# Two feed-forward layers on one Trainium2 core: sums taken off GpSimd, and the last two pairs of units multiplied with eight products

## The chip, the cores and the metric

The kernel runs on one core of one Trainium2 chip. The metric is the device time of one execution in microseconds (us). Before the change, three runs took 548.48, 549.16 and 550.05 us; the median is 549.16 us. A measurement of this kernel tells a change from no change at about 0.3%, 1.6 us.

The engines are named as the profile names them: PE is TensorE's matmul and PEld its weight load, DVE is VectorE, ACT is ScalarE, POOL is GpSimd, SP is SyncE, which issues the plain DMAs. The DMAs that add to their destination are issued by POOL.

## The reference

What is computed is causal attention over 2 x 12 heads of 448 positions and 64 channels, then two feed-forward layers over the 896 tokens (d_model 768, d_ff 2048). The weights arrive as 8-byte floats.

```python
x = attention(q, k, v)                      # causal, softmax, (896, 768)
h = x @ moe_w_in;  x = (h * cos(h)) @ moe_w_out
h = x @ moe2_w_in
g = where(h >= 1, h, where(h <= -1, 0, (h + 1) ** 2 / 4))
out = g @ moe2_w_out
```

## The kernel before, in words

**Order of work.** Attention follows a hand-written list of steps (STEPS). Then come four feed-forward stages: stage 1, `stage_in_plain` (x @ moe_w_in, plain products); stage 2, `stage_out(0)` (first moe_w_out); stage 3, `stage_in_split` (moe2_w_in); stage 4, `stage_out(1)` (second moe_w_out, whose results are the output, stored transposed). The class `Steps` records every operation of these stages with its engine, an assumed cost and the buffers that it reads and writes; `Plan.run` searches 300 rounds for an order and then emits the instructions of all engines in that order. Each engine and each queue runs its own instructions strictly in the emitted order. TensorE's order is the one in which the products are recorded.

**Products.** Every f32 operand is split into a high part in fp32r (ACT, `cast`, line 709 or, negated, 711) and a low rest (DVE, `rest`, line 718 or, negated, 720); one product is three matmuls per 128 rows: high-high, high-low, low-high. Stages 2 to 4 use a scheme with seven block products in place of eight, for which sums of blocks of the weights and of the activations are formed first. Stages 2 and 4 have 28 products of 18 matmuls each (7 products, `p`, times 4 slices, `j`), line 1013. Stage 3 walks over eight pairs of units g = 0..7 (128 columns of d_ff each); a pair has seven products of 9 matmuls, line 1275. Stages 2, 3 and 4 have 504 matmuls each, all of 128x128 by 448 columns.

**Weights.** A unit or a row block of 768 KB is loaded by SP into a raw buffer (line 333 or 807). ACT turns the top 16 bits of every weight into fp16 (`decode_top`, line 347); DVE joins them with the next bits to an f32 word (`decode_bits`, line 357), for units in place, in every second word of the raw buffer (`middle`). Half of each decoded row block is then negated on POOL (`minus`, line 821).

**Sums.** Those on POOL use `combine` (line 703): in stage 3 four sums S1 to S4 of 128x384 per pair (`sums` in `group`); in stages 2 and 4 the activation sums T1 (stage 4 also T2 and T3) of 128x896 and the weight sums S1 of 128x768, one per slice; between stages 2 and 3 nine differences of 128x448 (`difference`: T1, T2, T3). T4 between the stages runs on DVE. The sums T2 to T4 and S2 to S4 that line 698 (`add_by_dma`) forms are DMAs that POOL issues and that add the source to the destination in SBUF.

**PSUM hand-overs.** Results are read out of PSUM by DVE (line 1050 in stages 2 and 4; line 703 with `g<-m,kept` in stage 3) or kept by ACT (lines 1039, 1287). A later product that accumulates in the same PSUM tile waits for such a read. The gate of stage 3 is two ACT operations (1305, 1308) and one on DVE (1311) for each 448 tokens.

**Buffers of stage 3.** Raw units turn over four slots (b3 to b6), so the load of pair g+2 waits for the last reader of pair g. The split weights of a pair lie in the slots w0 to w3, one of each.

```python
go((1, 0), (5, 0), (6, 0), (2, 0), (7, 0))              # pair 0: (product, pair)
early = [(3, g - 1), (6, g), (4, g - 1)]                # pairs 1 to 7
go((1, g), (2, g), *early, (5, g), (7, g))
```

## Time and profile before

| | |
|---|---|
| median of the runs | 549.16 us (548.48 to 550.05) |
| the profiled execution | 550.65 us, span of its instructions 548.9 us |
| PE, PEld busy | 517.1 us (94%), 445.4 us (81%) |
| DVE busy | 425.8 us (78%) |
| ACT busy | 350.8 us (64%) |
| POOL busy | 232.5 us (42%) |
| TensorE's granted clock, mean | 0.981 of 2.4 GHz |
| a 768 KB unit from issue to landing, median | 4.7 us |
| decode of a unit, mean | ACT 1.08 us, DVE 1.07 us |
| casts on ACT, mean | 0.89 us (128x768), 0.57 us (128x448), 0.54 us (128x384) |
| the chain that ended last | PE 66%, DVE 20%, issue 6%, ACT 5%, POOL 2% |

Busy shares are means over the span; matmuls are pipelined, so TensorE's pace is read from the starts of successive matmuls and not from its busy share. A timeline row merges neighbouring instructions of one kind; `[4.18 <-DVE c L1050]` says that the engine stood idle for 4.18 us before it and that the DVE instruction of line 1050 that writes `c` ended this. Instructions of ACT and DVE overlap by about 0.1 us at their ends, so a row's length is a little more than what it adds to the engine's time. In the view of busy times by stretch, (x86) counts instructions, PEclk is TensorE's granted clock as a share of 2.4 GHz.

### The profile page before, as it was taken

The numbers are of one execution on the slowest core, as the hardware profiler recorded it, in microseconds if no ns is written. First come the engines' busy times: TensorE is split into PE (matmuls) and PEld (weight loads), VectorE is DVE, ScalarE is ACT, GpSimd is POOL, SyncE is SP. The second block draws the span as 40 slices with busy tenths as digits, with TensorE's granted clock in tenths as the row PEclk, the third lists the DMA queues.
The fourth block names the chain that finished last, engine by engine and source line by source line (L and its number), as shares of the span: only waits on it lengthen the run. The fifth ranks groups of instructions, "written<-read, shape, count | busy, mean of one in ns | idle before, by whom it ended". The sixth has DMA issues, their size and how long they took to land.

```text
span 548.9 us, 7642 instructions
## 1 busy us (share of the span) xinstructions
PE 517.1 (94%) x2792; PEld 445.4 (81%) x2792; DVE 425.8 (78%) x518; ACT 350.8 (64%) x599; POOL 232.5 (42%) x238
## 2 busy tenths in 40 slices
PE   8999999999999999999988979999999978899997
PEld 4666779989898988989877968898888767799886
DVE  7879775776766465997699976879899899997652
ACT  5998975866765465545475558777877665644340
POOL 4856641121201017770167062546485867770000
PEclk9999999999999999999997989999999988899999
DMA  8753309799842565665330334333359464792111
GB/s 267 261 177 124 94 3 320 219 301 289 270 108 74 132 158 93 123 119 99 116 115 1 115 97 152 98 115 110 121 144 312 141 182 146 153 203 54 50 51 51
DMA packets 42405, 79.01 MB, mean 144 GB/s; under 512 B 2432, under 2 KB 31616, under 8 KB 42368
## 3 DMA queue, kind: packets, MB, share of 16 engines
q1 hardware_dynamic: 36464, 61.51, 33.8%
q0 software_dynamic: 5760, 16.78, 16.7%
q8 instruction: 22, 0.36, 0.3%
q10 hardware_dynamic: 144, 0.23, 0.1%
q14 instruction: 15, 0.12, 0.1%
HBM read 58.98 MB, written 2.75 MB: 112 GB/s over the span
## 4 chain that ended last, share of the span: by engine, by line
PE 66%; DVE 20%; issue 6%; ACT 5%; POOL 2%; DMA 1%; DVEq 0%; ACTq 0%
PE m L1013 25%; PE m L851 19%; PE m L1275 7%; PE o L544 4%; PE m L591 2%; PE sa L431 2%; POOL raw L703 2%; PE tx L518 2%; PE sb L431 1%; PE tz L518 1%; DVE raw L357 1%; PE tw L518 1%; DVE g1.3.1_3746 L1311 1%; DVE w1g L718 1%; ACT top L347 1%
## 5 line engine op out<-in xcount | busy, mean ns | idle before, releaser
L851 PE MATMUL m<-x,w 128*128 128x384 f32 (+2 forms) x516 | 105.3, 366 | 0.0
L851 PEld LDWEIGHTS m<-x,w 128*128 128x128 f32 x516 | 93.4, 188 | 11.6
L703 POOL TENSOR_TENSOR raw<-raw 128x384 f32<-128x384 f32 x24 | 40.0, 1668 | 49.4 <-DVE raw L357 31.7
L347 ACT CAST top<-raw 128x768 f16<-128x768 bf16 x32 | 34.6, 1082 | 10.2 <-DMA raw<-in_moe_w_in 8.3
L357 DVE SCALAR_TENSOR_TENSOR raw<-raw,top 128x768 uint32<-128x768 uint32 x32 | 34.1, 1065 | 8.7 <-ACT top L347 8.7
L1275 PE MATMUL m<-rx,w2g 128*128 128x448 f32 x144 | 32.6, 370 | 3.6 <-ACT kept L1287 1.3
L1275 PE MATMUL m<-rx,w0g 128*128 128x448 f32 x144 | 32.4, 378 | 3.3 <-DVE w0g L718 3.3
L1275 PE MATMUL m<-rx,w1g 128*128 128x448 f32 x144 | 32.0, 368 | 2.3 <-DVE g1.1.0_3225 L703 1.2
L1275 PEld LDWEIGHTS m<-rx,w2g 128*128 128x128 f32 x144 | 26.7, 189 | 8.1 <-ACT kept L1287 2.1
L1275 PEld LDWEIGHTS m<-rx,w0g 128*128 128x128 f32 x144 | 28.1, 196 | 5.9 <-DVE w0g L718 3.6
L1275 PEld LDWEIGHTS m<-rx,w1g 128*128 128x128 f32 x144 | 26.7, 188 | 5.9 <-issue 1.6
L703 POOL TENSOR_TENSOR c<-c,c 128x448 f32<-128x448 f32 x9 | 15.0, 1682 | 29.7 <-issue 25.2
L1050 DVE TENSOR_TENSOR c<-m,p 128x448 f32<-128x448 f32 x24 | 14.5, 617 | 15.7 <-PE m L1013 15.6
L498 POOL TENSOR_SCALAR p<-p,rb 128x256 f32<-128x256 f32 (+1 forms) x32 | 18.1, 577 | 19.8 <-DVE rb L484 14.8
L544 PE MATMUL o<-pT,v 128*64 128x448 f32 (+3 forms) x192 | 23.2, 385 | 0.9 <-ACT pT L535 0.9
L498 POOL TENSOR_SCALAR p<-p,ra 128x384 f32<-128x384 f32 (+1 forms) x48 | 22.1, 479 | 3.2 <-ACT p L476 1.2
L1287 ACT COPY kept<-m 128x448 f32<-128x448 f32 x24 | 12.6, 526 | 16.3 <-PE m L1275 14.3
L544 PEld LDWEIGHTS o<-pT,v 128*64 128x64 f32 x192 | 12.6, 136 | 12.0 <-issue 6.3
L709 ACT CAST rx<-c 128x448 fp32r<-128x448 f32 x20 | 10.8, 567 | 11.7 <-DVE c L1050 10.0
L718 DVE TENSOR_TENSOR w1g<-raw,w1g 128x768 fp32r<-128x768 f32 x8 | 13.6, 1704 | 3.5 <-ACT w1g L709 3.5
L476 ACT ACTIVATE p<-sb,nmb 128x256 f32<-128x256 f32 x24 | 11.2, 476 | 7.1 <-DVE nmb L457 4.1
L476 ACT ACTIVATE p<-sa,nma 128x384 f32<-128x384 f32 x24 | 13.8, 584 | 1.8 <-DVE nmd L455 1.1
(639 smaller groups left out, 1443.3 us busy)
## 6 DMA issues: line engine op xcount, KB each, us to landing
raw<-in_moe_w_in SPq DMA_DIRECT2D x32, 768.0 KB, 4.7
v<-in_v SPq DMA_DIRECT2D x12, 256.0 KB, 5.7
k<-in_k SPq DMA_DIRECT2D x12, 224.0 KB, 5.1
out<-c SPq DMA_DIRECT2D x12, 224.0 KB, 1.9
qr<-in_q SPq DMA_DIRECT2D x11, 224.0 KB, 5.2
...
```

Source lines behind the costliest of these rows:

```text
L347: nc.scalar.copy(out=top.bitcast(FP16).rearrange("p (m e) -> p m e", e=2)[:, :, 1], in_=raw.bitcast(BF16)[:, 4:].rearrange("p (m e) -> p m ...
L357: nc.vector.scalar_tensor_tensor(out=fl, in0=bits, scalar=13, in1=top, op0=ALU.logical_shift_right, op1=ALU.bitwise_or,)
L431: nc.tensor.matmul(s[:, j, o : o + w], self.q[rows(n, j), i * QB : w], self.k[rows(n, j), :w], start=(o == 0), stop=False,)
L476: nc.scalar.activation(out=o, in_=i, func=AF.Exp, bias=nm[:, m : m + 1], scale=1.0 if n else scale, accum_out=self.r[r][:, c : c + 1],)
L498: e.tensor_scalar(out=p, in0=p, scalar1=r[:, c : c + 1], scalar2=1.0, op0=ALU.mult, op1=ALU.mult)
L518: nc.tensor.transpose(o, i, ident)
L544: nc.tensor.matmul(self.o[heads(j), c * QB : S], self.v[:, j, c, :], self.pT[:, c, j, c * QB :], start=(c == 0), stop=(c == FULL),)
L703: make = lambda: e.tensor_tensor(out=to(), in0=a(), in1=b(), op=op)
L718: nc.vector.tensor_tensor(out=to(), in0=what(), in1=f32(hi()), op=ALU.subtract)
L851: nc.tensor.matmul(o, w[:, a, c * P : (c + 1) * P], x(t, c)[:, s], start=(c == first and n == 0), stop=(c == last and n == 2),)
L1013: nc.tensor.matmul(o, wt[:, a, i * MW + d * P : i * MW + (d + 1) * P], r[:, i], start=(p in (0, k, 2, 4) and j == 0 and i == 0 and n == 0) ...
L1275: nc.tensor.matmul(o, wt[:, l, block, c * P : (c + 1) * P], rt[:, s, x], start=(n in (1, 2, 5) and c == 0 and e == 0), stop=(c == ML - 1 a ...
```

## The change

1. No arithmetic on POOL in the feed-forward stages. T1, T2, T3 and S1 of stages 2 and 4 move to DVE. Of stage 3's four sums per pair two move to DVE (new S2, S3), and two become adding DMAs (S4, S1). The sums between stages 2 and 3 (T1 to T4) become one adding DMA each over 128x1344; for that `c21` and `c12` are stored negated, and the pieces made from them are split with a sign. `minus` goes: the top half of a row block is decoded by two ACT operations, the second with a factor of -1; the second unit of a pair is decoded negated.
2. Decoded words of units are packed into the first words of the raw buffer (`words`) and no longer lie in every second word; the two sums E0, E1 follow behind them.
3. The pairs 6 and 7 of stage 3 (`CLASSIC`) use eight products with R11, R12, R21, R22 and no sums (`plain_product`); three new pieces R12 and two new slots for them (e0, e1).
4. Products of pairs 1 to 5 come in a new order; a gate takes two blocks in one instruction where both are ready. Row blocks and sums of stage 4 get other slots; the buffer for the descriptors of POOL's DMAs shrinks to 4096 bytes.

```diff
+    def decode_top(top, raw, sign=1, half=None):
...
+        if sign > 0:
+            nc.scalar.copy(out=to, in_=what)
+        else:
+            nc.scalar.mul(out=to, in_=what, mul=-1.0)
...
-        plan.op(
-            f"{k}a{n}", "ACT", 1.08, lambda: decode_top(tops[1], tile_of(name)), [(name, 0)], [("top1", 0)],
-        )
+        for half, sign in enumerate((1, -1)):
+            plan.op(
+                f"{k}a{n}.{half}", "ACT", 0.66, lambda half=half, sign=sign: decode_top(tops[1], tile_of(name), sign, half),
+                [(name, 0)], [("top1", half)],
+            )
...
-        plan.op(f"{k}g{n}", "POOL", 0.75, minus, [(ws, (1, i))], [(ws, (1, i))])
...
         def g_combine(name, j, to, a, b, op):
             combine(
-                f"{k}{name}.{j}", "POOL", 2.3, lambda: g_part(k, j, to), lambda: g_part(k, j, a), lambda: g_part(k, j, b),
+                f"{k}{name}.{j}", "DVE", 1.1, lambda: g_part(k, j, to), lambda: g_part(k, j, a), lambda: g_part(k, j, b),
...
-                    f"{k}S1.{j}", "POOL", 2.0, lambda j=j: ws_part(k, j, 0), lambda j=j: ws_part(k, j, 0),
+                    f"{k}S1.{j}", "DVE", 0.96, lambda j=j: ws_part(k, j, 0), lambda j=j: ws_part(k, j, 0),
...
+    def sum_of(name, to, what):
+        add_by_dma(
+            f"1d{name}", lambda: tile_of(to), lambda: tile_of(what),
+            [(t, c) for t in (to, what) for c in range(ML)], [(to, c) for c in range(ML)],
+        )
...
-            for d in range(ML):
-                difference("T1", "c210", "c210", "c220", ALU.subtract, d)
+                piece("R12", d, "c210", -1)
+            sum_of("T1", "c210", "c220")
+            sum_of("T2", "c110", "c220")
...
-            for d in range(ML):
-                difference("T4", "c110", "c120", "c110", ALU.subtract, d, "DVE")
+            sum_of("T4", "c110", "c120")
...
         def sums():
-            for u in (u0, u1):
-                decode(u)
-            for name, to, x, y, op in (
-                ("S1", (a, "B0"), (b, "A1"), (b, "A0"), ALU.add), ("S3", (b, "B0"), (a, "A1"), (b, "A1"), ALU.subtract),
-                ("S2", (a, "B1"), (a, "B0"), (a, "A1"), ALU.subtract), ("S4", (b, "B1"), (a, "A0"), (a, "B1"), ALU.subtract),
-            ):
-                combine(f"1{name}g{g}", "POOL", 1.2, half(*to), half(*x), half(*y), op, [x, y], [to])
+            decode(u0)
+            if g in CLASSIC:
+                decode(u1)
+                return
+            decode(u1, -1)
+            for name, to, x, y in (("S3", (a, "E0"), (a, "A1"), (b, "A1")), ("S2", (a, "E1"), (a, "E0"), (b, "A0"))):
+                combine(f"1{name}g{g}", "DVE", 0.55, half(*to), half(*x), half(*y), ALU.add, [x, y], [to])
...
             if n == 1:
                 fractions("w0", "w0", a, "A")
+                sum_by_dma("S4", (a, "A0"), (a, "E1"))
+                sum_by_dma("S1", (b, "A1"), (b, "A0"))
...
+        SUMS = {
+            "C12": ("y", 0, (("w0", 1, "R12"), ("w0", 0, "R22"))), "C11": ("xz", 0, (("w0", 1, "R11"), ("w0", 0, "R21"))),
+            "C21": ("y", 1, (("w2", 1, "R11"), ("w2", 0, "R21"))), "C22": ("xz", 1, (("w2", 0, "R22"), ("w2", 1, "R12"))),
+        }
...
-                go((1, g), (2, g), *early, (5, g), (7, g))
+            if g in CLASSIC:
+                steps = [(name, n, g) for name in ("C12", "C11", "C21", "C22") for n in range(2)]
+                steps[3:3] = pending[1:]
+                steps[1:1] = pending[:1]
+                pending = []
+            else:
+                if g == 0:
+                    steps = [(1, 0), (5, 0), (6, 0), (2, 0), (7, 0)]
+                else:
+                    steps = [(1, g), *pending, (6, g), (2, g), (7, g), (5, g)]
+                pending = [(4, g), (3, g)]
...
-        ["b0", "b2", "b0", "b2", "x14", "x5", "b0", "b2", "x14", "x5", "b1", "b0", "b2", "x14", "b1", "b0"],
+        [f"b{(0, 2, 1)[n % 3]}" for n in range(KF)],
...
-    nc = bacc.Bacc("TRN2", target_bir_lowering=False, num_devices=1)
+    nc = bacc.Bacc("TRN2", target_bir_lowering=False, num_devices=1, dynamic_dma_scratch_size=4096)
```

## Rows read from the trace of the kernel before

**Rows 1.** Busy time of each engine in four stretches of the feed-forward stages. Columns: see first line.
```profile
core 0: us, PE busy (x) PEld busy (x) DVE busy (x) ACT busy (x) POOL busy (x), PEclk, DMA share, GB/s
200.20:310.90 110.70, 105.04 (x506) 96.20 (x505) 93.17 (x86) 63.75 (x87) 53.27 (x38) 0.97 0.45 97
310.90:422.20 111.30, 102.90 (x488) 91.76 (x487) 94.64 (x112) 82.90 (x132) 58.92 (x38) 0.98 0.45 139
422.20:481.00 58.80, 50.21 (x217) 43.38 (x216) 56.08 (x44) 37.11 (x50) 45.38 (x33) 0.91 0.61 168
481.00:549.00 68.00, 62.47 (x307) 57.11 (x306) 42.29 (x47) 24.25 (x29) 10.02 (x8) 0.99 0.33 80
```

**Rows 2.** Chain of waits, pieces in order of time: start us, us, what.
```profile
454.55 2.87 DVE ws1.0.1_4017 L357
...
476.13 34.07 PE m L1013 x160
```

**Rows 3.** TensorE timeline of stage 2: start us, us, operands, count, [idle before <-releaser].
```profile
269.40 1.36 PE L1013 MATMUL m<-sx0.18_2632,sw0.18_2607 128*128 128x448 f32 x6
...
275.20 3.81 PE L1013 MATMUL m<-sx0.20_2683,sw0.20_2659 128*128 128x448 f32 x18
...
284.85 1.36 PE L1013 MATMUL m<-sx0.22_2742,sw0.22_2733 128*128 128x448 f32 x6
...
290.39 2.61 PE L1013 MATMUL m<-sx0.23_2773,sw0.23_2751 128*128 128x448 f32 x6 [4.18 <-DVE c L1050]
...
296.46 3.81 PE L1013 MATMUL m<-sx0.24_2805,sw0.24_2784 128*128 128x448 f32 x18
```

**Rows 4.** VectorE timeline of stage 2.
```profile
243.52 0.94 DVE L718 TENSOR_TENSOR sw0.13_2475<-ws0.1.1_1866,sw0.13_2475 128x768 fp32r<-128x768 f32 x1
...
264.57 1.09 DVE L718 TENSOR_TENSOR sx0.19_2657<-g0.3.0_2072,sx0.19_2657 128x896 fp32r<-128x896 f32 x1 [1.69 <-ACT sx0.19_2657 L709]
...
285.93 2.04 DVE L720 SCALAR_TENSOR_TENSOR sx0.24_2805<-g0.0.1_1442,sx0.24_2805 128x896 fp32r<-128x896 f32 x1
287.89 1.91 DVE L718 TENSOR_TENSOR sw0.25_2808<-ws0.1.1_1866,sw0.25_2808 128x768 fp32r<-128x768 f32 x1
289.73 0.61 DVE L1050 TENSOR_TENSOR c<-m,p 128x448 f32<-128x448 f32 x1
```

**Rows 5.** GpSimd timeline of stage 2.
```profile
243.69 1.84 POOL L698 DMA_DIRECT2D ws0.2.1_2030<-ws0.2.0_1569  x1
...
285.48 3.52 POOL L703 TENSOR_TENSOR raw<-raw 128x384 f32<-128x384 f32 x2
```

**Rows 6.** TensorE timeline, stage 3's start and stage 4's first product.
```profile
310.92 1.98 PE L1275 MATMUL m<-rx,w0g 128*128 128x448 f32 x9
...
318.99 2.10 PE L1275 MATMUL m<-rx,w2g 128*128 128x448 f32 x9 [0.62 <-ACT kept L1287]
...
324.75 5.07 PE L1275 MATMUL m<-rx,w0g 128*128 128x448 f32 x16 [3.25 <-DVE w0g L718]
...
332.45 2.08 PE L1275 MATMUL m<-rx,w1g 128*128 128x448 f32 x9 [0.78 <-DVE g1.0.0_3062 L703]
...
422.18 3.87 PE L1013 MATMUL m<-sx1.0_3827,sw1.0_3777 128*128 128x448 f32 x18
```

**Rows 7.** TensorE timeline of stage 4.
```profile
481.04 3.16 PE L1013 MATMUL m<-sx1.11_4199,sw1.11_4212 128*128 128x448 f32 x15
...
537.46 3.76 PE L1013 MATMUL m<-sx1.26_4585,sw1.26_4576 128*128 128x448 f32 x18
541.07 3.83 PE L1013 MATMUL m<-sx1.27_4611,sw1.27_4595 128*128 128x448 f32 x18
```

**Rows 8.** Busy time and granted clock in one stretch of stage 4, columns as in rows 1.
```profile
450.60:456.50 5.90, 5.90 (x17) 5.29 (x18) 5.90 (x3) 2.62 (x4) 5.90 (x3) 0.55 0.54 173
```

**Rows 9.** All fractions of half a unit on VectorE: ns min/median/max.
```profile
L718 DVE TENSOR_TENSOR w3g<-raw,w3g x8: 543/548/1107, 315.4 to 413.1; 128x384 fp32r<-128x384 f32 x8
```

**Rows 10.** All adding DMAs of the program, from issue to landing.
```profile
DMA to landing us min/median/max: 3.9/5.8/10.3
```

More of the change, by code (lines that the diff above doesn't have):

```diff
@@ L343, in middle, with words @@
         return raw.bitcast(U32)[:, : 2 * UW].rearrange("p (m e) -> p m e", e=2)[:, :, 1]
-    def decode_top(top, raw):
-        nc.scalar.copy(
-            out=top.bitcast(FP16).rearrange("p (m e) -> p m e", e=2)[:, :, 1],
-            in_=raw.bitcast(BF16)[:, 4:].rearrange("p (m e) -> p m e", e=4)[:, :, 0],
-        )
+    def words(raw):
+        return raw.bitcast(U32)[:, :UW]
+    def decode_top(top, raw, sign=1, half=None):
+        to = top.bitcast(FP16).rearrange("p (m e) -> p m e", e=2)[:, :, 1]
+        what = raw.bitcast(BF16)[:, 4:].rearrange("p (m e) -> p m e", e=4)[:, :, 0]
+        if half is not None:
+            part = slice(half * (UW // 2), (half + 1) * (UW // 2))
+            to, what = to[:, part], what[:, part]
+        if sign > 0:
+            nc.scalar.copy(out=to, in_=what)
+        else:
+            nc.scalar.mul(out=to, in_=what, mul=-1.0)
     def decode_bits(fl, top, raw):
-        bits, top = middle(raw), top
+        bits = middle(raw)
         if len(fl.shape) == 3:
@@ L365, in decode_unit @@
         yield
-        decode_bits(middle(raw), tops[0], raw)
+        decode_bits(words(raw), tops[0], raw)
         yield
-        fl = middle(raw).bitcast(F32)
+        fl = words(raw).bitcast(F32)
         ready[u] = w = place(f"w{u}", f"w{u}", [P, 2, UW], F32R)
@@ L870, in gate @@
             g = g_buf(0, j, q // 2)
-            gp = [(g, (0, i)), (g, (1, i))]
+            gp = [(g, (n, i)) for n in range(2)]
             hp = [(f"h{f}", 0), (f"h{f}", 1)]
@@ L921, in stage_in_plain @@
                     buf(w, f"w{u % 4}", [P, 2, UW], F32R)
-                    words = [(raw, "A0"), (raw, "A1")]
-                    fl = lambda raw=raw: middle(tile_of(raw)).bitcast(F32)
+                    need = [(raw, "A0"), (raw, "A1")]
+                    fl = lambda raw=raw: words(tile_of(raw)).bitcast(F32)
                     hi = lambda w=w: tile_of(w)[:, 0]
                     lo = lambda w=w: tile_of(w)[:, 1]
-                    cast(f"H{u}", 0.88, hi, fl, words, [(w, "h")])
-                    rest(f"O{u}", 0.96, lo, fl, hi, words + [(w, "h")], [(w, "l")])
+                    cast(f"H{u}", 0.83, hi, fl, need, [(w, "h")])
+                    rest(f"O{u}", 0.96, lo, fl, hi, need + [(w, "h")], [(w, "l")])
                     bank_buf(f"h{u}")
@@ L1049, in make @@
                 ob = tile_of(c)
-                nc.vector.tensor_tensor(
-                    out=ob[:, d], in0=bank(k, f"{chain}{d}"), in1=tile_of(f"{old}{k}")[:, d], op=ALU.add
-                )
+                one, two = bank(k, f"{chain}{d}"), tile_of(f"{old}{k}")[:, d]
+                if k == 0 and name in ("c21", "c12"):
+                    nc.vector.scalar_tensor_tensor(
+                        out=ob[:, d], in0=one, scalar=-1.0, in1=two, op0=ALU.mult, op1=ALU.subtract
+                    )
+                else:
+                    nc.vector.tensor_tensor(out=ob[:, d], in0=one, in1=two, op=ALU.add)
                 if k:
@@ L1261, in product @@
             if block is None:
-                w, block = f"w3g{g // 2}", g % 2
+                w, block = "w3g", g % 2
                 left = [(w, (p, block)) for p in LETTERS]
@@ L1295, in result, with gate @@
             )
[L1297 to L1300 removed]
+        def gate(qs, direct=None):
+            n, q = len(qs), qs[0]
+            gp = [a for q in qs for a in g_access(1, j, q, i)]
+            to = lambda: tile_of(gp[0][0])[:, :, i] if n == 2 else g_part(1, j, q)[:, i]
+            h, hp = to, gp
+            ax = lambda: tile_of("kept")[:, ML - 1 :] if n == 2 else tile_of("kept")[:, ML]
+            axp = [("kept", ML - 1 + m) for m in range(2)][2 - n :]
             if direct:
[L1302 removed]
+                h, hp, ax, axp = *direct, to, gp
             def relu():
@@ L1361, in go @@
         def go(*steps):
-            for n, g in steps:
-                last[g](n)
+            for *n, g in steps:
+                last[g](*n)
         ready_group(0)
```

174 lines of the change are left out of this document (95 added, 79 removed), and 2 rows, old and new, of the table PIECES.

## The prediction

> **What bounds the kernel now.** I looked first at busy time by stretch [rows 1]: TensorE is busy 95, 92, 85 and 92% of the four, VectorE 84, 85, 95 and 62%, and in the third stretch the granted clock is only 0.91. Then the chain of waits: from about 360 us to 476 us its pieces are nearly all VectorE's and ScalarE's, such as a decode that took 2.87 us, and only from 476 us is it TensorE's alone again [rows 2]. So TensorE sets the end in most of the program, and VectorE in the second half of stage 3 and the first of stage 4.
>
> How much TensorE loses is read from starts of matmuls. Undisturbed, 18 of them take 541.07 - 537.46 = 3.61 us, 0.2006 each [rows 7]. Against that pace:
>
> - Stage 2, 284.85 to 296.46: 24 matmuls, 4.81 us, in 11.61: 6.8 lost [rows 3].
> - Stage 3's start, 310.92 to 332.45: 72 matmuls (five products of pair 0, two of pair 1, one more of pair 0), 14.44 in 21.53: 7.1 lost [rows 6].
> - The rest of stage 3, 332.45 to 422.18: 414, 83.05 in 89.73: 6.7 lost [rows 6].
> - First part of stage 4, 422.18 to 481.04: 216 (18 are left over from stage 3), 43.33 in 58.86: 15.5 lost [rows 6, 7].
>
> That is 36 us. Each loss has the wait itself and, after a long wait, some 16 matmuls at half pace: after the longest wait of stage 4 the granted clock is 0.55, close to 1.2 of 2.4 GHz [rows 8]; the 16 matmuls at 324.75 take 5.07 us [rows 6].
>
> **Why VectorE is late.** In stage 2 TensorE waits 4.18 us for the result that VectorE writes at 289.73 [rows 3, 4]. Ahead of it stand operations of 2.04 and 1.91 us that take 1.09 and 0.94 us at other times [rows 4], and GpSimd adds without a break meanwhile [rows 5]. The result itself, which reads PSUM and SBUF, takes 0.61 in the middle of this. So operations with both inputs in SBUF take about twice as long beside GpSimd's arithmetic. While GpSimd only issues adding DMAs (243.69), VectorE's operation at 243.52 takes 0.94 us [rows 4, 5]: issuing doesn't stretch it.
>
> **Part 1: GpSimd's arithmetic goes.** What VectorE gets: 16 T sums and 8 weight sums, two half sums for each of six pairs, three R12 rests, less three T4 differences. By [rows 4, 9]: stage 2, 4 x 1.09 + 4 x 0.94 = 8.1 us; stage 3, 12 x 0.55 = 6.6, R12 against T4 nothing; stage 4, 12 x 1.09 + 4 x 0.94 = 16.8. What it gets back is the stretching. In the first part of stage 4 an instruction takes 56.08 / 44 = 1.27 us, afterwards, with little arithmetic on GpSimd, 42.29 / 47 = 0.90 [rows 1]: 44 x 0.37 = 16 us there alone. Stage by stage along the path:
>
> - Stage 2: the hand-over shrinks to what the same one costs where VectorE is on time, 269.40 to 275.20, 24 matmuls in 5.80, 0.99 lost [rows 3]. Gain 6.8 - 1.0 = 5.8. The 8.1 us of new work lie early, in a stage with 17 us of idle VectorE. Bounds 4 and 6.8.
> - Stage 3's start: the 3.25 us wait for w0 and its slow matmuls [rows 6] end in VectorE's queue behind stretched work. The 0.62 us wait for `kept` stays, since product 6 to 7 leaves ScalarE one product as before. I leave 2.5 of 7.1; gain 4.6, bounds 2 and 6.2.
> - First part of stage 4: VectorE's 56.1 us become 56.1 - 16 + 13.1 (T1 to T3) = 53; three of the eleven decodes there can come earlier (the row slots of stage 3's end and two light pairs allow it), -2.8, and T1, which product 20 needs first, can wait, -4.4: 45.8. At the 95% to which VectorE fills this stretch now it would last 48.2; with half of the T1 there, 50.5. I take 49.4, a gain of 9.5. Bounds: all but one hand-over gone, 14.5; below, a loss of 4, if decodes and sums crowd it.
> - S1, deferred there, falls into the last stretch, where VectorE is 62% busy [rows 1]: nothing, covered by 25 us of idle time; its losses there are hand-overs that stay.
>
> **The adding DMAs.** Sixteen are added (two in each of six pairs, four between the stages). GpSimd's queue holds then only issues, each waiting for its source; nobody waits for GpSimd except through the landing. An add takes 3.9 to 10.3 us to land [rows 10]. The sharpest is T4: it can start when c12 is complete, three results of 0.61 [rows 4] or about 2 us into stage 3, and its product is the seventh, after 6 x 1.81 + 0.6 = 11.5 us; the split of three pieces (casts of 0.57, then a rest) takes about 2.4. So 7.1 us are there: no wait at 3.9, 3.2 us at 10.3. I take 0.5 at the typical 5.8 (it moves 672 KB, half as much again as the largest so far), and have it in the 2.5 above. The Trainium skill's "DMA: Bandwidth & Descriptors", section on the anatomy of one DMA, gives 2.0 us plus bytes over 436 GB/s, which I estimate at 3.6 us for T4: the sum would be 0.5 lower; the shortest of the 44 rows is longer than that though smaller, so the rows decide. In the pairs the chain is: S4 lands (4 to 10), w3 split 1.3 (two of 0.55 and a hand-over), load 4.7 at the median and say 9.4 at worst, decode of both units and sums 4.2, w0 split 2: 16 to 27 us, typically 18, and hand-overs, against 25.3 for two pairs of seven products.
>
> **Part 2: packed words.** VectorE's rest of a strided half unit takes 0.543 to 0.548 undisturbed [rows 9], 384 elements; a contiguous 768 takes 0.94 [rows 4]. Per element that is the same but for a fixed part, so packing gives nothing by itself; bounds 0 and 1 us.
>
> **Part 3: eight products in two pairs.** 2 x 9 matmuls more, 18 x 0.2006 = 3.6 us on TensorE, in full on the path. VectorE loses there one and a half splits, three results and half the gates, about 3.6 us a pair, which makes room for the row decodes. No leftover products of stage 3 remain to lie between the first of stage 4.
>
> **Part 4: new order.** In pairs 1 to 7 products 6 and 3 often wait for a read of VectorE out of the same PSUM tile, as product 6 does at 332.45 for that of product 2's half, 0.78 us [rows 6]; seven such waits, none above 1.3 us, stand in the stage. Now 6 comes before 2, and the read that 3 waits for no longer waits for ScalarE's copy of product 7: most of them go. Against it, w0 of the next pair may be split only after product 2, which leaves 3.6 us in place of 9 for a cast, a rest and two hand-overs, some 2.4. I leave 3.7 of 6.7: gain 3.0; bounds 6.2 and a loss of 1. A row block's two half casts are put down at 2 x 0.66 us against 1.08 before, 0.24 more for each of 32; ScalarE is idle for a quarter of stage 3 and longer elsewhere [rows 1], so nothing; without that cover 7.7 us.
>
> **Sum.** 5.8 + 4.6 + 9.5 + 3.0 - 3.6 = 19.3 us. The profiled execution took 550.65 us, so 531.3; the median of the runs is 1.5 lower, 549.16, so 529.9: I say 530. Ends: 6.8 + 6.2 + 14.5 + 6.2 + 1 - 3.6 = 31 gives 518; 4 + 2 - 4 - 1 - 3.6 = -2.6 the other way round is 2.6 slower, 552, but the bad ends are unlikely together. With the last two at their bad ends and the others as taken, 549.2 - 5.8 - 4.6 + 4 + 1 + 3.6 = 547.
>
> **Rivals.**
>
> - *VectorE stays the bound from pair 6 to product 16 of stage 4.* For it: 95% busy there, and 13 us of sums come. If no decode moves and T1 isn't put off, 53 / 0.95 = 56 us, a gain of 3 in place of 9.5: 536.
> - *The adds land late.* Loads of 768 KB share the DMA engines. At 10.3 us every time and 9.4 for loads two pairs take 27 and 3 of hand-overs in place of 25.3, three times: 14 us, and T4's 2.7 more: 547. Against it: the DMA engines are only 45% busy in stage 3 [rows 1], and 5.8 is typical.
> - *Slower: VectorE's long operations aren't due to GpSimd's arithmetic.* If they come from elsewhere, say from the DMA traffic, then VectorE keeps 56 us and gets 13 more in stage 4's first part: 69 / 0.95 = 73 in place of 58.9, 14 more, plus 3.6 of matmuls, with no gain but order's 3.0: 564. It decides where such operations stay above 1.2 us with GpSimd quiet; 243.52 speaks against it [rows 4].
> - *It changes nothing*, if the search finds a poor order; its waits were unforeseen before, too.
>
> **How the numbers follow.** Forecast 0.68, VectorE the bound 0.13, late adds 0.09, no change 0.03, slower 0.07 (the stretching 0.04, poor order 0.03). Faster by over 0.3%, which is about what a measurement of this kernel can tell, is 0.68 + 0.13 + 0.09 = 0.90; within it 0.03; slower 0.07. The range, 520 to 545, takes in the forecast but its luckiest end, the first rival and most of the second.
>
> **What would show it.** Right: VectorE's two-input operations at 0.95 and 1.09 us everywhere, no row of arithmetic on GpSimd after attention, no wait of TensorE above 1.5 us in stages 2 to 4, a granted clock near 1.0, the first part of stage 4, counted as eleven products, near 46 us, stage 3 near 111 us with 522 matmuls. Wrong: VectorE above 95% between pair 6 and product 16 with waits behind it; waits for `w3g` or for raw units behind adds; long operations beside a quiet GpSimd.

## The result and the profile after

The kernel after takes 528.55 us (median of four runs, 528.35 to 529.92), the kernel before 549.61 us on the same chip: ratio 0.9617, 95% interval 0.9583 to 0.9652, so faster by 3.8%. The profiled execution took 528.35 us, its span is 526.4 us.

**By stage.** What TensorE loses in a stage is read as in the prediction: the time from its first matmul to the first of the next stage, less 0.2006 us for each matmul between them. The starts for after stand in the timeline below, those for before in [rows 3, 6, 7]; stage 2 begins at 199.82 and 200.31.

| lost by TensorE, us | before | after | the prediction left |
|---|---|---|---|
| stage 2 (504 matmuls) | 9.5 | 3.2 | 3.7 |
| stage 3 up to stage 4's first (486, after 522) | 13.8 | 10.4 | 6.2 |
| stage 4, first eleven products (216, after 198) | 15.5 | 0.1 | 6.0 |
| stage 4, product 11 to the last one's start (288) | 2.3 | 2.3 | 2.3 |

With 3.6 us for 18 more matmuls, and 0.5 us less ahead of stage 2, this makes 6.3 + 3.4 + 15.4 + 0.5 - 3.6 = 22.0 of the 22.3 us between the two profiled executions.

Of the page of after, the first line of the busy times and the chain of waits by engine:

```profile
PE 509.2 (97%) x2810; PEld 442.4 (84%) x2810; DVE 383.9 (73%) x534; ACT 344.3 (65%) x604; POOL 96.2 (18%) x157
...
PE 94%; DVE 3%; ACT 1%; issue 1%; DVEq 0%
```

The chain was 66% TensorE and 20% VectorE before; now it is TensorE's nearly alone. Busy times of after in the four stretches that answer to [rows 1], with the same columns:

```profile
core 0: us, PE busy (x) PEld busy (x) DVE busy (x) ACT busy (x) POOL busy (x), PEclk, DMA share, GB/s
199.80:304.10 104.30, 102.25 (x505) 94.29 (x504) 82.71 (x101) 64.35 (x90) 17.27 (x21) 1.00 0.62 135
304.10:419.20 115.10, 108.58 (x524) 97.23 (x523) 84.15 (x114) 82.86 (x124) 11.91 (x14) 1.00 0.62 172
419.20:459.00 39.80, 39.80 (x200) 37.05 (x199) 35.97 (x40) 30.16 (x44) 8.75 (x11) 1.00 0.90 226
459.00:526.40 67.40, 62.40 (x307) 57.00 (x305) 42.64 (x51) 24.25 (x29) 2.37 (x3) 1.00 0.26 68
```

In the second and third stretch VectorE is busy 73% and 90%, where it was 85% and 95%, although the sums are now its own; the granted clock is 1.00 throughout, 0.91 before in the third. POOL's instructions here only issue DMAs. TensorE's timeline of after, as [rows 3, 6, 7]:

```profile
285.94 1.48 PE L1019 MATMUL m<-sx0.23_2777,sw0.23_2750 128*128 128x448 f32 x6 [0.72 <-DVE c L1062]
...
304.10 1.98 PE L1283 MATMUL m<-rx,w0g 128*128 128x448 f32 x9
...
312.18 2.10 PE L1283 MATMUL m<-rx,w1g 128*128 128x448 f32 x9 [0.62 <-ACT kept L1295]
...
315.86 1.69 PE L1283 MATMUL m<-rx,w0g 128*128 128x448 f32 x7 [1.18 <-DVE w0g L726]
...
321.03 2.00 PE L1283 MATMUL m<-rx,w1g 128*128 128x448 f32 x9
322.87 1.98 PE L1283 MATMUL m<-rx,w0g 128*128 128x448 f32 x9
325.47 2.10 PE L1283 MATMUL m<-rx,w1g 128*128 128x448 f32 x9 [0.62 <-ACT kept L1295]
...
419.17 3.81 PE L1019 MATMUL m<-sx1.0_3701,sw1.0_3803 128*128 128x448 f32 x18
...
458.99 3.25 PE L1019 MATMUL m<-sx1.11_4137,sw1.11_4187 128*128 128x448 f32 x14
...
519.11 3.76 PE L1019 MATMUL m<-sx1.27_4566,sw1.27_4550 128*128 128x448 f32 x18
```

The wait of 4.18 us in stage 2 [rows 3] is now 0.72; that of 3.25 us in stage 3 [rows 6] is 1.18; stage 4's first eleven products run at TensorE's pace. What TensorE still waits for from stage 2 on, in sums (us in total, times, longest), the four largest:

```profile
PE m L1283 <- ACT kept L1295: 3.7, 6, 0.6
PE m L1019 <- DVE c L1062: 2.2, 3, 0.7
PE m L1283 <- DVE w0g L726: 1.6, 3, 1.2
PE m L1283 <- DVE w2g L726: 1.2, 1, 1.2
```

The first line has grown: six times 0.62 us, once in each of the pairs 0 to 5. The kernel before had two such waits, but there six others stood in stage 3 behind VectorE's reads of results (`g1`), 3.7 us in all, of which none is left:

```profile
PE m L1275 <- ACT kept L1287: 1.3, 2, 0.7
PE m L1275 <- DVE g1.1.0_3225 L703: 1.2, 1, 1.2
...
PE m L1275 <- DVE g1.2.1_3526 L703: 0.8, 2, 0.6
```

Two VectorE operations of stage 2, and all rests of half a unit in stage 3 (ns min/median/max), as [rows 4, 9]:

```profile
223.65 1.09 DVE L726 TENSOR_TENSOR sx0.8_2360<-g0.0.1_1442,sx0.8_2360 128x896 fp32r<-128x896 f32 x1
224.66 0.95 DVE L726 TENSOR_TENSOR sw0.9_2363<-ws0.1.1_1924,sw0.9_2363 128x768 fp32r<-128x768 f32 x1
```
```profile
L726 DVE TENSOR_TENSOR w3g<-raw,w3g x6: 551/552/557, 307.4 to 386.4; 128x384 fp32r<-128x384 f32 x6
```

None of these operations is stretched any more; the rests reached 1107 ns before. The DMAs of after (KB each and median us to landing; and, as in [rows 10], all adding DMAs together):

```profile
c<-c POOLq DMA_DIRECT2D x4, 672.0 KB, 6.5
raw<-raw POOLq DMA_DIRECT2D x12, 192.0 KB, 4.3
...
DMA to landing us min/median/max: 3.5/5.9/11.4
```

No row of TensorE's waits in after names an add.

### The profile page after: what moved, and what is told of

The parts are those of the page before. It is cut to its first block, busy times and chain, and to the rows that moved or that the text cites. A ratio compares the mean times of both kernels' runs of the same rounds, so it can differ in the third digit from the quotient of the medians.

```text
span 526.4 us, 7606 instructions
## 1 busy us (share of the span) xinstructions
PE 509.2 (97%) x2810; PEld 442.4 (84%) x2810; DVE 383.9 (73%) x534; ACT 344.3 (65%) x604; POOL 96.2 (18%) x157
## 4 chain that ended last, share of the span: by engine, by line
PE 94%; DVE 3%; ACT 1%; issue 1%; DVEq 0%
PE m L1019 39%; PE m L857 20%; PE m L1283 14%; PE m L1382 6%; PE o L552 4%; PE m L599 2%; PE sa L439 2%; PE tx L526 2%; PE sb L439 1%; PE tz L526 1%; PE tw L526 1%; PE warm L624 1%; ACT kept L1295 1%; DVE raw L365 1%; PE sc L424 1%
## 5 line engine op out<-in xcount | busy, mean ns | idle before, releaser
L356 ACT CAST top<-raw 128x768 f16<-128x768 bf16 x26 | 27.9, 1075 | 8.3 <-DMA raw<-in_moe_w_in 7.7
L1283 PE MATMUL m<-rx,w1g 128*128 128x448 f32 x108 | 24.6, 372 | 3.7 <-ACT kept L1295 3.7
L1283 PE MATMUL m<-rx,w0g 128*128 128x448 f32 x108 | 24.6, 367 | 1.6 <-DVE w0g L726 1.6
L1283 PEld LDWEIGHTS m<-rx,w1g 128*128 128x128 f32 x108 | 19.8, 188 | 7.5 <-ACT kept L1295 6.0
L1283 PEld LDWEIGHTS m<-rx,w0g 128*128 128x128 f32 x108 | 20.0, 188 | 4.2 <-DVE w0g L726 2.8
L706 POOL DMA_DIRECT2D raw<-raw x12 | 10.2, 851 | 69.2 <-DVE g1.0.1_3110 L1322 14.6
L552 PEld LDWEIGHTS o<-pT,v 128*64 128x64 f32 x192 | 12.6, 136 | 12.0 <-issue 6.3
L506 POOL TENSOR_SCALAR p<-p,rb 128x256 f32<-128x256 f32 (+1 forms) x32 | 18.1, 577 | 20.4 <-DVE rb L492 15.5
L1283 PE MATMUL m<-rx,w2g 128*128 128x448 f32 x90 | 20.4, 365 | 1.2 <-DVE w2g L726 1.2
L1283 PEld LDWEIGHTS m<-rx,w2g 128*128 128x128 f32 x90 | 16.8, 188 | 2.9 <-DVE w2g L726 1.6
L484 ACT ACTIVATE p<-sa,nma 128x384 f32<-128x384 f32 x24 | 13.8, 583 | 1.4 <-DVE nmd L463 0.7
L726 DVE TENSOR_TENSOR w<-raw,w 128x768 fp32r<-128x768 f32 x14 | 13.3, 950 | 0.9 <-ACT w L717 0.9
L439 PE MATMUL sa<-k,q 64*128 64x384 f32 (+1 forms) x88 | 12.4, 401 | 0.4 <-ACT p L484 0.4
```

What stands on the lines that cost most here:

```text
L356: nc.scalar.copy(out=to, in_=what)
L439: nc.tensor.matmul(s[:, j, o : o + w], self.q[rows(n, j), i * QB : w], self.k[rows(n, j), :w], start=(o == 0), stop=False,)
L484: nc.scalar.activation(out=o, in_=i, func=AF.Exp, bias=nm[:, m : m + 1], scale=1.0 if n else scale, accum_out=self.r[r][:, c : c + 1],)
L506: e.tensor_scalar(out=p, in0=p, scalar1=r[:, c : c + 1], scalar2=1.0, op0=ALU.mult, op1=ALU.mult)
L552: nc.tensor.matmul(self.o[heads(j), c * QB : S], self.v[:, j, c, :], self.pT[:, c, j, c * QB :], start=(c == 0), stop=(c == FULL),)
L1283: nc.tensor.matmul(o, wt[:, l, block, c * P : (c + 1) * P], rt[:, s, x], start=(n in (1, 2, 5) and c == 0 and e == 0), stop=(c == ML - 1 a ...
```

## The experiments

Twelve kernels, each run beside the kernel before on the same chip; the median of the kernel before was 548.72 to 549.61 us there, so the times of the rows can be compared with each other to about 1 us. Starts and losses as in the table above; "first eleven" is stage 4 up to product 11.

| run | us, median (range) | lost in stage 2 | stage 3 | first eleven | rest |
|---|---|---|---|---|---|
| after | 528.55 (528.35 to 529.92) | 3.2 | 10.4 | 0.1 | 2.3 |
| t_s1_on_gpsimd | 541.1 (540.49 to 541.71) | 4.1 | 13.1 | 10.0 | 2.1 |
| before_t_s1_on_vectore | 532.94 (531.65 to 534.24) | 8.7 | 8.8 | 4.0 | 3.2 |
| idle_adds | 550.73 (one) | 9.0 | 12.2 | 7.4 | 10.0 |
| idle_writes | 527.22 (one) | 3.5 | 8.7 | 0.0 | 2.0 |
| one_pair_of_eight | 532.89 (532.62 to 533.05) | 3.0 | 12.2 | 4.9 | 2.1 |
| three_pairs_of_eight | 528.24 (528.03 to 530.04) | 3.2 | 8.8 | 0.0 | 2.0 |
| sums_on_vectore | 533.13 (531.58 to 533.28) | 6.6 | 10.1 | 0.0 | 2.2 |
| old_order | 536.42 (533.14 to 537.89) | 3.0 | 19.4 | 0.0 | 2.1 |
| six_five_seven | 522.98 (522.03 to 523.72) | 3.0 | 5.4 | 0.0 | 2.1 |
| three_tiles | 518.29 (518.09 to 520.17) | 0.6 | 5.7 | 0.0 | 0.0 |
| three_tiles_one_pair | 525.38 (524.75 to 526.07) | 0.4 | 9.0 | 4.1 | 2.3 |
| pair_0_too | 521.94 (520.71 to 522.9) | 0.4 | 7.3 | 0.0 | 1.8 |

### Was it GpSimd's arithmetic that stretched VectorE?

**t_s1_on_gpsimd** takes one part of the change back, as below; **before_t_s1_on_vectore** makes that part alone, by the opposite edit in the kernel before:

```diff
-                f"{k}{name}.{j}", "DVE", 1.1, lambda: g_part(k, j, to), ...
+                f"{k}{name}.{j}", "POOL", 2.3, lambda: g_part(k, j, to), ...
...
-                    f"{k}S1.{j}", "DVE", 0.96, ...
+                    f"{k}S1.{j}", "POOL", 2.0, ...
```

> One part of the change undone: the 16 T sums and 8 weight sums of stages 2 and 4 run on GpSimd again, all else as in the changed kernel. If VectorE was late because GpSimd's arithmetic stretched its two-input operations, the 24 sums (about 2.4 us each, 58 us of GpSimd) stretch such operations again in stages 2 and 4, up to 3 us each, stage 3 stays at 115 us, and the time rises by 5 to 15 us, to 534 to 544, although VectorE has 25 us less to do. If the work itself is what counts, VectorE is freer than in the changed kernel and the time stays within 1 us of 528.5 or falls.

> The kernel before, with the T and S1 sums of stages 2 and 4 alone moved from GpSimd to VectorE; the four sums per pair in stage 3, the differences and the negations stay on GpSimd. Theory (the T and S1 sums were most of what stretched VectorE in stages 2 and 4): stage 2 loses 1 to 3 us instead of 6.8, the first part of stage 4 some 8 instead of 15.5, stage 3 stays as it was: 535 to 542. Rival (the gain needs all of GpSimd's arithmetic gone, and the twelve sums just load VectorE where it is the bound): 546 or more.

The first took 541.1 us (ratio 0.9856, 0.9835 to 0.9878), 12.6 more than after; 9.9 us of it are lost in the first eleven products and 2.7 in stage 3, which was expected to stay. VectorE and GpSimd there:

```profile
432.42 2.88 DVE L365 SCALAR_TENSOR_TENSOR ws1.0.1_3925<-rows1.8_3809,top 128x768 uint32<-128x768 uint32 x1
435.22 1.08 DVE L728 SCALAR_TENSOR_TENSOR sx1.4_3923<-g1.1.0_3251,sx1.4_3923 128x896 fp32r<-128x896 f32 x1
...
437.09 2.88 DVE L365 SCALAR_TENSOR_TENSOR ws1.0.1_3925<-rows1.9_3839,top 128x768 uint32<-128x768 uint32 x1
```
```profile
431.64 2.84 POOL L711 TENSOR_TENSOR g1.2.1_3526<-g1.2.0_3461,g1.2.1_3526 128x896 f32<-128x896 f32 x1
436.44 2.71 POOL L711 TENSOR_TENSOR g1.1.0_3251<-g1.1.1_3316 128x896 f32<-128x896 f32 x1 [1.97 <-DVE sx1.4_3923 L728]
```

GpSimd's two sums end at 434.48 and 439.15; the decodes beside them end at 435.30 and 439.97, both 0.82 us later, and take 0.95 alone. So do 12 of the 13 decodes and splits of this width that begin inside one of this run's sums, by 0.81 to 0.83 us. One that began at 436.22, just before GpSimd's sum at 436.44, took 0.95. So VectorE does not run at half speed: an operation that comes second stands until GpSimd's instruction is over, and then does nearly all of its own.

The second took 532.94 us (ratio 0.97, 0.9665 to 0.9734): moving these sums alone gives 16.5 us, where the whole change gives 21. It is quicker than expected, and not where it was expected. The first eleven products lose 4.0, where I had some 8. Stage 3, which was to stay, gained 5.0 (13.8 to 8.8), probably because GpSimd formed three of stage 4's T sums there before (at 352.9, 381.3 and 409.1). Stage 2 hardly gained (9.5 to 8.7): its hand-over still waits 4.20 us, because the additions beside it are those of stage 3's first pairs, as [rows 5] show by their name (`raw<-raw`), and they were left on GpSimd.

**idle_adds** and **idle_writes** put 144 instructions whose result nobody uses on GpSimd in the kernel after, two beside every split of stages 2 and 4 and four beside every pair of stage 3; the kernels' other work is unchanged.

```diff
+        nc.gpsimd.tensor_tensor(out=idle, in0=idle, in1=idle, op=ALU.add)     # idle_adds
+        nc.gpsimd.memset(idle, 0.0)                                           # idle_writes
```

> The changed kernel with additions on GpSimd that nobody reads: two of 128x384, a tile added to itself, beside each of the 56 products of stages 2 and 4 and each unit of stage 3. VectorE's list is that of the changed kernel. If arithmetic on GpSimd that reads SBUF is the cause, VectorE's operations with two inputs in SBUF grow from 0.95 and 1.09 us to 1.5 to 3 us where they meet it, those that read PSUM stay at 0.62, TensorE waits again, and the time is 540 to 565. If what helped is only that nobody waits for GpSimd's sums any more, the time stays at 528 to 531 and VectorE's operations keep their lengths.

> As the run with idle additions, but GpSimd fills the tile with zeros in place of adding: it writes SBUF and reads nothing. If VectorE and GpSimd meet at reading, VectorE's operations stay at 0.95 and 1.09 us and the time at 528 to 531. If any GpSimd instruction stretches them, they grow as with the additions, and the time rises by more than 3 us.

The additions cost 22 us, the writes nothing (527.22). GpSimd, and the same kind of VectorE operation beside it, in idle_adds and then in idle_writes:

```profile
215.03 2.75 POOL L707 TENSOR_TENSOR idle<-idle 128x384 f32<-128x384 f32 x2
...
217.02 1.58 DVE L735 TENSOR_TENSOR sw0.6_2329<-ws0.2.0_1574,sw0.6_2329 128x768 fp32r<-128x768 f32 x1
```
```profile
218.64 1.22 POOL L707 MEMSET idle<- 128x384 f32 x2
...
219.60 0.95 DVE L735 TENSOR_TENSOR sw0.7_2352<-ws0.3.0_1712,sw0.7_2352 128x768 fp32r<-128x768 f32 x1
```

Beside additions the rest again ends 0.82 us after GpSimd (217.78 and 218.60); beside writes it takes 0.95 as ever. VectorE's reads of one PSUM and one SBUF operand stay at 0.61 to 0.63 us in both. GpSimd also issues the adding DMAs, which stand behind the additions in its queue, but that can be a small part of the cost only: in the chain of waits of idle_adds VectorE has 31% of the span, where it has 3% in after, and GpSimd and the DMAs have 1% each, where they have none. The Trainium skill's "SBUF — State Buffer", section "Who interferes with whom", says that a VectorE instruction with two SBUF inputs contends with a GpSimd instruction that reads SBUF and not with one that only writes, and that the order of issue decides which of the two blocks. Both runs agree, with 1.58 against 0.95, and so does t_s1_on_gpsimd, with 2.88 for the operations that came second and 0.95 for the one that came first. The prediction's rival, that something else stretches VectorE, falls.

What these runs leave open is stage 3's own share. The chain of waits of before also passes through GpSimd's half sums themselves, 5.28 us for three at 362.90 and 5.27 for three at 390.09; VectorE now forms such a sum in 0.55 us where GpSimd took 1.67. No run moves the sums of stage 3, the differences or the negations alone.

### What the eight products give

**one_pair_of_eight** and **three_pairs_of_eight** change the kernel after, **three_tiles_one_pair** the kernel three_tiles below:

```diff
-    CLASSIC = (6, 7)
+    CLASSIC = (7,)        # one_pair_of_eight, three_tiles_one_pair
+    CLASSIC = (5, 6, 7)   # three_pairs_of_eight
```

> The kernel after, with eight products in pair 7 only; pair 6 has seven products and sums again. 9 matmuls less, 1.8 us, and about 3.6 us more for VectorE in stage 3. Theory (VectorE, 73% busy in stage 3 and done with 7 of the 12 T sums there, has room for it; the second eight-product pair costs its matmuls and gives nothing): 526 to 527.5, with stage 4's first eleven products still at 40 to 41 us. Rival (the eight products are what lets stage 3's VectorE take the T sums and decodes of stage 4): 529 to 533, with the loss at the end of stage 3 or in the first products of stage 4.

> three_tiles with eight products in pair 7 only. Theory (the second pair relieves VectorE, which hands stage 4 a later start on its decodes and sums when it is missing, whatever the order): stage 4's first eleven products take 43 to 46 us instead of 39.75, stage 3 saves 1.8 us, 520.5 to 523. Rival (in one_pair_of_eight an unlucky order of ScalarE's and VectorE's work made the 4.8 us, not their load): 516.5 to 517.5, with the eleven products at 40 us.

> The kernel after, with eight products in pairs 5, 6 and 7. Theory (the second pair of eight paid because VectorE was the bound in stage 4's first eleven products; with two pairs these take 39.8 us, 0.1 more than their 198 matmuls, so nothing is left to gain there): 9 matmuls more, 1.8 us, less the 0.9 us wait for kept that pair 5 has now: 529 to 530.5. Rival (every such pair pays 6 us, as the second one did: 4.3 us in time and 1.8 us of matmuls): 522 to 525.

My theory for the first fell: 532.89 us (ratio 0.9698, 0.9684 to 0.9713), 4.3 more than after with 9 matmuls less. The first eleven products of one_pair_of_eight and of three_pairs_of_eight, columns as in [rows 1]:

```profile
419.30:463.90 44.60, 41.89 (x199) 38.28 (x198) 41.40 (x46) 33.95 (x52) 9.00 (x11) 0.96 0.97 261
```
```profile
419.80:459.50 39.70, 39.70 (x199) 37.10 (x198) 35.71 (x40) 27.87 (x40) 9.43 (x11) 1.00 0.80 186
```

With one pair VectorE has 46 operations there instead of 40, and the DMA engines are 97% busy. The reason lies in stage 3. The first decoded weights of stage 4, `ws1.0.0`, take, by the kernel's lists of slots, the slot (x7) of pieces that product 7 reads. So their decode waits for the last product 7, which belongs to pair 5 in after and to pair 6 in one_pair_of_eight. This product 7 on TensorE and the decode on VectorE, first of after, then of one_pair_of_eight:

```profile
381.14 2.10 PE L1283 MATMUL m<-rx,w1g 128*128 128x448 f32 x9 [0.62 <-ACT kept L1295]
...
387.96 0.95 DVE L365 SCALAR_TENSOR_TENSOR ws1.0.0_3603<-rows1.0_3093,top 128x768 uint32<-128x768 uint32 x1
```
```profile
396.77 2.10 PE L1283 MATMUL m<-rx,w1g 128*128 128x448 f32 x9 [0.62 <-ACT kept L1295]
...
402.72 0.95 DVE L365 SCALAR_TENSOR_TENSOR ws1.0.0_3703<-rows1.0_3083,top 128x768 uint32<-128x768 uint32 x1
```

The decode comes 15 us later, and the loads that wait for the row block's slot with it; seven row blocks are decoded before stage 4 in after, four in one_pair_of_eight. In both runs ScalarE had made the top halves for this first decode by 330 us, so what it waits for is not its data; no run gives it another slot. three_tiles_one_pair shows the same from another start: 43.8 us for the eleven, and 525.38 us (ratio 0.9566, 0.9524 to 0.9609), 7.1 more than three_tiles and above the expected 520.5 to 523, as stage 3 lost 3.3 more and the rest of stage 4 another 2.3. A third pair changes nothing (528.24, ratio 0.9626, 0.9588 to 0.9664): the eleven are at TensorE's pace already, and 1.8 us of matmuls are paid back by 1.6 us less lost in stage 3. So the second pair is worth 6.1 us (4.3 and its 1.8), where the prediction priced only VectorE's operations. TensorE's one long wait in the eleven products of one_pair_of_eight is before and inside product 10, 1.76 and 0.95 us, for the weights of `ws1.2.1`, TensorE and then VectorE:

```profile
457.38 0.68 PE L1019 MATMUL m<-sx1.10_4111,sw1.10_4156 128*128 128x448 f32 x2 [1.76 <-ACT sw1.10_4156 L717]
...
455.26 0.95 DVE L365 SCALAR_TENSOR_TENSOR ws1.2.1_4103<-rows1.13_4056,top 128x768 uint32<-128x768 uint32 x1
```

Its last row block had landed at 450.0 and was decoded at 455.26, and VectorE had work without a break from 449.98: here VectorE's queue comes last, and not the load.

**sums_on_vectore** forms S4 and S1 of stage 3 with `combine` on VectorE in place of the adding DMAs.

```diff
-                sum_by_dma("S4", (a, "A0"), (a, "E1"))
-                sum_by_dma("S1", (b, "A1"), (b, "A0"))
+                for name, to, x in (("S4", (a, "A0"), (a, "E1")), ("S1", (b, "A1"), (b, "A0"))):
+                    combine(f"1{name}g{g}", "DVE", 0.55, half(*to), half(*to), half(*x), ALU.add, [to, x], [to])
```

> The kernel after, with S4 and S1 of pairs 0 to 5 in stage 3 formed by VectorE (12 operations of 0.55 us, 6.6 us) and not by adding DMAs. Theory (VectorE's work in stage 3 and in stage 4's first products is one budget: what it gets in the one, it is late with in the other): stage 4's first eleven products grow from 39.8 to 42 to 46 us, 531 to 535. Rival A (24 us of idle VectorE in stage 3 take it): 527.5 to 529.5. Rival B (the adds land late and cost waits in stage 3, which go): 523 to 527, with fewer waits in stage 3.

The time falls into the theory's range, 533.13 (ratio 0.9702, 0.9664 to 0.9739), and the theory is wrong: the eleven products lose nothing, and stage 3 loses 10.1 where after loses 10.4. So VectorE has the room, as rival A says, and no wait for a late add went, against rival B. Most of the time, 3.4 us, went into a hand-over at the end of stage 2, TensorE first, then VectorE, then ScalarE:

```profile
287.65 1.90 PE L1019 MATMUL m<-sx0.23_2770,sw0.23_2752 128*128 128x448 f32 x6 [2.66 <-DVE c L1062]
```
```profile
284.25 0.63 DVE L726 TENSOR_TENSOR rx<-c,rx 128x448 fp32r<-128x448 f32 x1 [2.12 <-ACT rx L717]
...
286.98 0.62 DVE L1062 TENSOR_TENSOR c<-m,p 128x448 f32<-128x448 f32 x1
```
```profile
283.65 0.57 ACT L717 CAST rx<-c 128x448 fp32r<-128x448 f32 x1 [3.96 <-DMA c<-c]
```

The result `c` stands in VectorE's queue behind a piece that waits 2.12 us for ScalarE, and behind two splits; and ScalarE stood 3.96 us for the first adding DMA between the stages (T3), issued at 276.11 and 7.5 us under way. In after the same add takes 7.2 us, but there `c` does not stand behind its piece. So a late add can cost a wait, by way of the order. No S4 or S1 stands there; the search has put the operations in another order. So the run bounds what the sums cost VectorE in place (nothing seen), and a range that is met says nothing without its mechanism.

### What the order gives

**old_order** has the order of before in the kernel after, **six_five_seven** another one; in both the result C22 is taken after product 7, which is now the last:

```diff
-                    steps = [(1, g), *pending, (6, g), (2, g), (7, g), (5, g)]
+                    steps = [(1, g), (2, g), (3, g - 1), (6, g), (4, g - 1), (5, g), (7, g)]   # old_order
+                    steps = [(1, g), (2, g), *pending, (6, g), (5, g), (7, g)]                 # six_five_seven
```

> Only the order of products in pairs 1 to 5 of stage 3: 1, 2, then 4 and 3 of the pair before, 6, 5, 7, in place of 1, 4, 3, 6, 2, 7, 5; the result C22 is taken after 7. In the changed kernel ScalarE's copy of product 6 starts only when product 2, which lies in the same PSUM tile, has ended, and product 7 then stands idle 0.62 us, some 0.9 with the first matmuls after it, in each pair. If the shared tile is the cause, product 5 (another tile) between 6 and 7 ends this wait in pairs 1 to 5, 0.9 us each, and the waits for w0 (0.5 in two pairs) end too, since product 2 frees w0 early: 523 to 525. If the copy itself is too slow for one product's length, the wait stays and the time is 528 to 529.

> The kernel after, with the order of products of before (1, 2, 3 and 6, 4, 5, 7) in pairs 1 to 5. Theory (the waits of the old order came from VectorE being late, not from the order; with one more product between 2 and 6 it is the better one now): the six kept waits of the new order go, as they did in six_five_seven, 523 to 526. Rival, the step of the prediction (the new order itself takes most of the waits away): 530 to 533, with waits of product 6 or 3 for reads by VectorE.

six_five_seven: 522.98 us, ratio 0.9527 (0.9508 to 0.9547); five of the six waits for `kept` are gone. Their cause is seen in ScalarE's timeline of after:

```profile
324.89 0.53 ACT L1295 COPY kept<-m 128x448 f32<-128x448 f32 x1 [1.83 <-PE m L1283]
```

Product 2 follows product 6 at 322.87 (timeline above), but ScalarE waits 1.83 us more, until product 2's matmuls end, too: products 6 and 2 write two halves of one PSUM tile, and a read waits for the whole tile. Then product 7, next in order and in 6's half, waits for the copy. With 5 between 6 and 7, in another tile, the copy is hidden.

old_order was worse than both theories had it, 536.42 (ratio 0.9753, 0.971 to 0.9797), for a third reason (its waits, columns as above):

```profile
PE m L1283 <- ACT w2g L717: 7.2, 5, 2.3
...
PE m L1283 <- DVE w2g L726: 1.6, 5, 0.3
```

In the kernel after products 4 and 5 read the two halves of `w2` (4 reads the old pair's, 5 the new one's), which products 3 and 7 did before. In the old order 5 follows 4 at once, so cast and rest of the new `w2` lie open. The old order's waits were for reads of results [rows 6]; they are not among these, although the order is the old one. So it does without them once VectorE is no longer stretched, if its waits for `w2` did not give VectorE the time. The order had to change with the slots, and this run cannot say what it alone is worth.

**three_tiles** moves sums that are filled in turn and stood in one PSUM tile apart, on top of six_five_seven, and in one product of stage 2 takes the three blocks in another order; **pair_0_too** adds another order of pair 0.

```diff
-        "x0": ("xa", 0), "x1": ("xa", 1), "x2": ("xb", 0), "z0": ("za", 0), "z1": ("za", 1), "z2": ("zb", 0),
-        "y0": ("za", 0), "y1": ("za", 1), "y2": ("zb", 1),
+        "x0": ("xa", 0), "x1": ("xb", 0), "x2": ("xa", 1), "z0": ("za", 0), "z1": ("za", 1), "z2": ("zb", 0),
+        "y0": ("za", 0), "y1": ("zb", 1), "y2": ("xb", 1),
...
-                for d in range(ML):
+                for d in (1, 0, 2) if (k, t) == (0, NJ) else range(ML):
...
-                    steps = [(1, 0), (5, 0), (6, 0), (2, 0), (7, 0)]
+                    steps = [(1, 0), (6, 0), (2, 0), (5, 0), (7, 0)]   # pair_0_too alone
```

> The order of six_five_seven, and in stages 2 and 4 the three sums that are filled in turn (x0 x1 x2, y0 y1 y2) lie in three different PSUM tiles instead of two of them in one. Theory (a wait counts for a whole PSUM tile: TensorE's five waits of 0.7 to 0.8 us with 0.1 us after each, four at products 18/19 and 22/23 and one at 2/3, come from a neighbour in the same tile being read): all five go, 5 x 0.9 = 4.6 us, so 522.98 - 4.6 = 518.4, say 517.5 to 519.5, and no wait of TensorE behind c or p above 0.3 us is left in stages 2 and 4. Rival (they are ScalarE and VectorE coming late with the read itself): 522 to 524 and the waits stay.

> three_tiles with pair 0's products in the order 1, 6, 2, 5, 7 instead of 1, 5, 6, 2, 7. Theory (the two waits left at stage 3's start have the same two causes as the others: product 7 comes right behind the copy of product 6's result, 0.62 us, and w0 is free for pair 1 only one product before it is wanted, 1.2 us): both go, 0.9 + 1.4 = 2.3 us with the slow matmuls behind them, 516.0, say 515.5 to 517. Rival (the pieces T2 and R21, which hang on the last result of stage 2, become what is late): 518 to 520, with waits behind rx at products 6 and 2.

three_tiles: 518.29 us, ratio 0.9441 (0.9419 to 0.9462), the best of all, 10.3 us under after. The five waits that six_five_seven still had in stages 2 and 4 for reads of results, 3.5 us in all, are gone; the hand-over that waited 4.18 us before and 0.72 after [rows 3] now runs through, a group of six every 1.20 us (the last row is cut off by the end of the view):

```profile
283.27 1.36 PE L1019 MATMUL m<-sx0.23_2777,sw0.23_2750 128*128 128x448 f32 x6
284.47 1.36 PE L1019 MATMUL m<-sx0.22_2745,sw0.22_2728 128*128 128x448 f32 x6
285.67 0.56 PE L1019 MATMUL m<-sx0.23_2777,sw0.23_2750 128*128 128x448 f32 x2
```

pair_0_too missed, 521.94 (ratio 0.9497, 0.947 to 0.9525). The wait for w0 went, but these two came in stage 3, and neither is the rival's:

```profile
303.83 2.10 PE L1283 MATMUL m<-rx,w1g 128*128 128x448 f32 x9 [0.62 <-ACT kept L1295]
...
310.99 2.08 PE L1283 MATMUL m<-rx,w1g 128*128 128x448 f32 x9 [1.40 <-DVE g1.0.0_3045 L711]
```

Product 1's result is kept as well, so 6 right behind 1 waits for that copy, as 7 behind 6 did; and product 7 waits for a read of a result that stands behind a decode in VectorE's queue. A third, 1.25 us at product 17 of stage 4, where VectorE now reads two results in a row, makes most of the 1.8 us in the last column.

## Why the prediction was right, and where not

The forecast of 530 us, 529.9 by its sum, is 1.5 us above the 528.55 measured, and its main mechanism is the one that the runs show. That it came so near is luck in part, since two errors nearly cancel: stage 4's first part gained 5.9 us more than forecast, the rest of stage 3 4.2 less.

- **VectorE is late because of GpSimd's arithmetic.** Right, by taking it back (12.6 us), putting it in alone (16.5) and adding unrelated arithmetic (22). "About twice as long" was the wrong form: VectorE stands until GpSimd's instruction ends. And from 360 to 476 us the chain is not nearly all VectorE's and ScalarE's: GpSimd's own sums hold 10.5 us of it, which the prediction did not price.
- **Stage 2**, gain 5.8 at one hand-over: that wait is 0.72 us, the stage gained 6.3. Right.
- **Stage 3's start**, 2.5 to be left of 7.1: 72 matmuls from 304.10 to 321.03 take 16.93, so 2.5 is left. The size is right, its parts only half: the 0.62 us for `kept` stays as said, but the wait for w0, which was to end, stays at 1.18 us. Not all of it came from stretched work: pair 0's order leaves one product between its last reader of w0 and pair 1's first, and with another order it goes (pair_0_too).
- **Part 4, the order**, 3.7 to be left of 6.7: wrong. From 321.03 to 419.17 stand 450 matmuls, 90.3 us in 98.1, so 7.9 is lost, 4.2 more than forecast, and a loss of 1.2 where a loss of 1 was the lower bound. The waits that were to go did go: of the seven, six were for VectorE's reads, 3.7 us, and one for a copy of ScalarE's; none of the six is left. But old_order has none of them either, so this looks like the work of a VectorE on time rather than of the order; no run settles it. The step that failed is the price of the new order, in which the sum had nothing but w0. The prediction saw that in pair 0 ScalarE has one product, 2, to copy 6's result before 7, and that this costs 0.62 us; the new order puts 6, 2, 7 in the same row in pairs 1 to 5, and the sum did not carry the wait there. Five of these are 3.1 us, with the slower matmuls behind each by my estimate some 4.5, and six_five_seven takes them back with 5.6 us in all. A wait for w2, 1.18 us once, was not foreseen, either.
- **First part of stage 4**, gain 9.5: 15.4 was measured. The step is the count of what falls into this stretch. I had 44 operations, 12 sums more, 3 decodes and 4 T1 less: 49. It is 40: the rows of after hold 5 T sums and not 8 (5 of the 12 lie in stage 3, not 7 as I put down for one_pair_of_eight, and two later), 20 splits and not 23, 5 reads and gates and not 10, against one decode and one S1 more. At 0.90 us each, 9 operations are 8 us; and at 36.0 us VectorE no longer bounds 39.8 us of matmuls, so the 95% rule that I took from before had no place. Part 3 moved much of it. I priced it by VectorE's own work; but it also ends the use of the sums' pieces one pair earlier, and with them frees stage 4's slots 15 us earlier: with one such pair the eleven products lose 4.9 us, near the 6.0 that I left.
- **18 matmuls**, 3.6 us: they are there in full, and by one_pair_of_eight the second nine give back 6.1 us for 1.8.
- **Packed words, half casts:** nothing, as said: a packed rest of half a unit takes 0.552 against 0.548 us [rows 9], and ScalarE is busy 30 of 39.8 us where the half casts of row blocks lie.
- **Adding DMAs:** T4's add takes 5.8 us, of four of 672 KB with a median of 6.5, and costs no wait, where I had 0.5. By the Trainium skill's "DMA: Bandwidth & Descriptors", section on the anatomy of one DMA, my estimate was 3.6; the median is nearly twice that. The rival of late adds falls for after: no wait of TensorE ends with one, and without the pairs' adds stage 3 loses as much (sums_on_vectore). That an add can be late is shown by the hand-over of sums_on_vectore, 2.66 us behind T3's.

Of the marks set beforehand these held: operations at 0.95 and 1.09 us, no arithmetic on GpSimd after attention, no wait above 1.5 us, a clock of 1.00. Two did not: 46 us for the eleven products (39.8) and 111 for stage 3 (115.1). Two slips in reading change no term: the adding DMAs of before are 40, not 44; and the 16 matmuls at 324.75, 5.07 us [rows 6], are not all at half pace, at which they would take 6.4, but about half of them.
